# One attention and Fourier kernel on one core: array shapes chosen in the order, score units of four head groups, masks over 16 heads

## The chip, the core and the metric

The kernel runs on one core of a Trainium2 chip. The core has five engines that work side by side: TensorE (matrix products, called PE in the profile, its weight loads PEld), VectorE (DVE), ScalarE (ACT), GpSimd (POOL) and SyncE (SP), which here only issues DMAs. The metric is the time of one execution on the device in microseconds.

## The reference

One input x (2048 tokens, 640 channels) goes through two branches, and a gate per token mixes them. All tensors are bf16.

```python
H, N = 32, 4                      # 32 heads of 20 channels, 4 segments of 512 tokens
q, k, v = x @ wq, x @ wk, x @ wv  # cut into heads and segments
M = z = 0
for s in range(N):
    p = softmax(qs @ ks.T * 20 ** -0.5 + causal_mask)      # inside the segment
    a_dot = p @ vs
    a_mem = (phi(qs) @ M) / (phi(qs) @ z + 1e-6)           # memory of the segments before
    o = sigmoid(beta) * a_mem + (1 - sigmoid(beta)) * a_dot
    M, z = M + phi(ks).T @ vs, z + phi(ks).sum()           # phi(t) = t + 1 if t > 0 else exp(t)
a = concat(o) @ wo
b = irfft2(rfft2(x) * (w_r + 1j * w_i))
out = sigmoid((x * gate_w).sum(-1)) * a + (1 - the same) * b
```

## The kernel before

`record` writes down some 2,300 operations (products, copies, activations, masks, DMAs) with what they read and write. `schedule` then puts them into engine queues by a long list of numbers, `ORDER`: an entry v means operation v // 2 on its first or second possible engine (v % 2). So the sequence on every engine, and the engine of each operation that has two, is written out in that list. `schedule` also assigns the PSUM banks and the semaphore waits, with a cost model of its own.

*Stages.* For each segment s, `project` computes q, k (`proj_tile`: 128 channels by 512 tokens, five products of 128x128), v (`v_tile`), and the token gate; the rows of q and k go through memory (`st_qk`, `pad`) to get 20-row heads onto 32-row strips (`qkp`). `mem_read` reads the memory, `attend` does the attention, `mem_update` adds to the memory. `fft` is the Fourier branch: `F1`, `D`, `T`, `W_mul`, `W_add`, `Tb`, `Db`. `finish_tile` makes output tiles out of `Fb` and five `oproj`, and `final` copies them out of PSUM. The order list mixes all of these: Fourier products fill the places between attention products.

*Scores.* Eight groups of four heads per segment. A unit of scores (`qk_unit`) is a set of products into PSUM banks 0 to 3, all four of them, then one exponential on ScalarE (L1271; two for some units of segment 3) into the tile `ex`, then causal masks on GpSimd (L1292). Kind a is the first block of keys, kind b the next two, kind c the last. The units of two groups are a, b, a, c (of both), b: 20 units per segment. `ex` has three slots, so the scores of a group go to the slot of the group three before, after its product with v (`pvf` in segments 0 to 2, `pv` in segment 3). All other products use PSUM banks 4 to 7.

*Array shapes.* TensorE works as one array of 128x128, as four column tiles of 128x32 (`pvf`, `Fb`, odd v tiles, `projd`, output products), or as eight tiles of 20x64 (scores). The first is mode 0, the second 2, the third 1. In the profile's shapes these are `128*128`, `128*32` and `20*64`. Only the output products of segments 0 to 2 (`oproj`, mode -1) could take either of the first two, by their neighbours in the list.

*Lines.* L522 issues most products, L520 a product cut into four tiles; L531 and L533 are the copies out of PSUM on ScalarE and VectorE; L1080, L1092 and L1093 are phi; L1121 the gate's exponential; L1452 `W_add`; L1447 `W_mul`.

## Time and profile before

| | |
|---|---|
| median of 3 runs | 245.5 us (244.65 to 246.56) |
| the profiled execution | 246.08 us in all; span from first to last instruction 244.0 us |
| mean granted TensorE clock | 0.993 of full speed |
| TensorE / VectorE / ScalarE / GpSimd busy | 226.9 / 200.7 / 200.4 / 167.2 us |
| DMA | 42.17 MB, 173 GB/s on average |

In a row of a group, the form reads out<-in with partitions x elements; after the count come the busy time in us, the mean length of one in ns, and the idle time just before with what ended it. In a row of the time-ordered list come the start, the length, the engine, the line and how many instructions are merged. The lengths of products are modelled and overlap; their starts are measured. In a row of stages, after the bounds and the length, come the busy times of PE, PEld, DVE, ACT and POOL with instruction counts, the granted clock, the DMA share and GB/s.

### The profile page before, as it was taken

How to read it: one execution, taken by the hardware profiler on the slowest of the kernel's cores; microseconds unless marked ns; L12 is line 12 of the kernel's file. 1: busy time of each engine (PE TensorE's matmuls, PEld its weight loads, DVE VectorE, ACT ScalarE, POOL GpSimd, SP SyncE). 2: the span in 40 equal slices, each digit the busy share in tenths (PEclk: the TensorE clock that was granted, in tenths of full speed). 3: DMA queues.
4: the chain of work that ended last, by engine and by line, in shares of the span. 5: the costliest groups of instructions: out<-in, count | busy, mean ns of one | idle time of the engine just before them, and what ended most of it. 6: DMA issues, size and time to landing. Idle time of an engine off the chain costs nothing.

```text
span 244.0 us, 10261 instructions
## 1 busy us (share of the span) xinstructions
PE 226.9 (93%) x4349; PEld 140.8 (58%) x4361; DVE 200.7 (82%) x478; ACT 200.4 (82%) x243; POOL 167.2 (69%) x298
## 2 busy tenths in 40 slices
PE   7999999999979999899799979998999989999994
PEld 2674666766455665455575545565554546566793
DVE  0299989889999987999997998998999996735473
ACT  2388989988989999899898879999999968687801
POOL 8334069447959938649779895968898783857730
PEclk9999999999999999999999999999999999799999
DMA  7999959996977975849637583463876759382213
GB/s 168 301 330 268 209 173 182 233 194 199 214 209 131 189 222 147 183 141 252 159 98 203 134 247 97 126 169 105 227 172 201 182 130 206 95 87 83 72 67 108
DMA packets 58928, 42.17 MB, mean 173 GB/s; under 512 B 30020, under 2 KB 55172, under 8 KB 58884
## 3 DMA queue, kind: packets, MB, share of 16 engines
q1 hardware_dynamic: 57188, 40.71, 67.9%
q10 hardware_dynamic: 1696, 0.82, 1.2%
q8 instruction: 34, 0.56, 1.0%
q14 instruction: 10, 0.08, 0.1%
HBM read 23.32 MB, written 12.30 MB: 146 GB/s over the span
## 4 chain that ended last, share of the span: by engine, by line
PE 63%; DVE 16%; ACT 10%; DMA 7%; issue 2%; ACTq 0%; SPq 0%; DVEq 0%
PE psum L522 57%; ACT ex L1271 8%; PE psum L520 5%; DMA r<-r_scr 2%; DMA xT<-in_A_x_dram 2%; DVE Yt L1452 2%; DVE Pt L1447 2%; DVE phk L1093 2%; DMA dnc<-u_scr 2%; DVE oU L1534 1%; DMA u_scr<-ub 1%; ACT et L1080 1%; DVE Cp L533 1%; DVE ub L533 1%; DVE G L1493 1%
## 5 line engine op out<-in xcount | busy, mean ns | idle before, releaser
L1271 ACT ACTIVATE ex<-psum 128x2048 bf16<-128x2048 f32 (+4 forms) x92 | 138.6, 1506 | 15.5 <-PE psum L522 13.1
L1292 POOL TENSOR_SCALAR_AFFINE_SELECT ex<-ex 128x256 bf16<-128x256 bf16 (+2 forms) x224 | 122.6, 570 | 35.3 <-ACT ex L1271 32.8
L522 PE MATMUL psum<-qkp 20*64 20x64 bf16 (+5 forms) x1280 | 32.7, 271 | 3.9 <-ACT ex L1271 2.9
L522 PE MATMUL psum<-xT,wk 128*128 128x256 bf16 (+1 forms) x280 | 33.8, 281 | 0.6 <-DMA xT<-in_A_x_dram 0.4
L522 PE MATMUL psum<-wv,xT 128*32 128x320 bf16 (+3 forms) x400 | 29.4, 301 | 0.0
L522 PE MATMUL psum<-xT,wq 128*128 128x512 bf16 (+1 forms) x123 | 28.0, 385 | 0.8 <-issue 0.5
L1447 DVE TENSOR_TENSOR Pt<-psum,Wt 128x642 bf16<-128x642 f32 x32 | 25.5, 821 | 0.6 <-PE psum L522 0.2
L522 PEld LDWEIGHTS psum<-qkp 20*64 20x64 bf16 x1280 | 13.4, 103 | 21.6 <-ACT ex L1271 15.1
L522 PEld LDWEIGHTS psum<-xT,wk 128*128 128x128 bf16 (+1 forms) x280 | 19.8, 99 | 8.3 <-issue 1.8
L520 PE MATMUL psum<-wo,oU 128*32 128x320 bf16 x480 | 22.2, 305 | 0.5 <-DVE oU L1542 0.2
L522 PE MATMUL psum<-big,Ac 128*128 128x161 bf16 (+2 forms) x96 | 17.6, 257 | 2.0 <-DVE va L1123 1.5
L522 PE MATMUL psum<-ex,va 128*32 128x64 bf16 (+3 forms) x576 | 17.6, 257 | 1.8 <-DVE Pt L1447 1.3
L522 PE MATMUL psum<-big,Cp 128*128 128x321 bf16 (+1 forms) x96 | 18.1, 307 | 1.0 <-DVE G L1493 0.6
L522 PEld LDWEIGHTS psum<-wv,xT 128*32 128x32 bf16 (+1 forms) x400 | 14.5, 96 | 7.4 <-issue 2.0
L1123 DVE TENSOR_TENSOR va<-psum,ebx 128x320 bf16<-128x320 f32 x32 | 15.3, 483 | 2.9 <-PE psum L522 1.8
L914 POOL TENSOR_TENSOR xsb<-xf 128x320 bf16<-128x320 bf16 (+2 forms) x9 | 7.6, 846 | 14.4 <-DVE xsb L914 10.3
L522 PEld LDWEIGHTS psum<-ex,va 128*32 128x32 bf16 x576 | 11.0, 96 | 10.7 <-DVE Pt L1447 2.2
L1493 DVE TENSOR_TENSOR G<-eo,psum 128x320 bf16<-128x320 f32 x32 | 14.9, 478 | 2.3 <-PE psum L522 1.9
L533 DVE CAST ot<-psum 128x320 bf16<-128x320 f32 x18 | 8.5, 488 | 9.8 <-PE psum L520 7.9
L1080 ACT ACTIVATE et<-qu 128x512 bf16<-128x512 bf16 x25 | 15.3, 625 | 0.9 <-DVE phk L1093 0.9
L522 PE MATMUL psum<-tt,Yt 128*128 128x256 bf16 (+1 forms) x96 | 15.6, 274 | 0.3 <-DVE mem L1165 0.2
L1452 POOL TENSOR_TENSOR Yt<-Pt 128x321 bf16<-128x321 bf16 x17 | 12.7, 758 | 4.4 <-PE psum L522 3.9
(96 smaller groups left out, 401.2 us busy)
## 6 DMA issues: line engine op xcount, KB each, us to landing
qkp<-qk_scr SPq DMA_DIRECT2D x28, 160.0 KB
tt<-tab_tt SPq DMA_DIRECT2D x8, 512.0 KB, 4.3
qk_scr<-qu SPq DMA_DIRECT2D x12, 256.0 KB, 3.0
u_scr<-ub SPq DMA_DIRECT2D x12, 256.0 KB, 3.1
xsb<-in_A_x_dram SPq DMA_DIRECT2D x8, 320.0 KB, 4.9
oU<-u_scr SPq DMA_DIRECT2D x15, 128.0 KB, 3.2
out_dram<-ot SPq DMA_DIRECT2D x12, 160.0 KB
Wt<-in_B_w_r_dram SPq DMA_DIRECT2D x16, 80.2 KB, 3.2
```

The source lines that it names most:

```text
L520: h = e.matmul(dst, wt, r_, start=st, stop=sp_, **{**kw, "tile_position": (0, q), "skip_group_check": True})
L522: h = e.matmul(o_, l_, r_, start=st, stop=sp_, **kw)
L533: alts["dve"] = (lambda e: e.tensor_copy(dst(), src()), 67 + 1.04 * n, 68.0)
L914: self.either(lambda e, dst=dst, src=src, d0=d0, n=n, op=op: e.tensor_tensor(xs.ap(o + dst, [D, 2], [1, n]), xf.ap(src + d0, [321, 2], [1, ...
L1080: self.one("act", lambda e: e.activation(et.ap(0, [1, L]), qsl(), ACT.Exp), L, [qb], [b("et", pi_)], late, name="phi_exp")
L1093: fmin = lambda e: e.tensor_tensor(dst(), dst(), et.ap(0, [1, L]), ALU.min)
L1123: self.one("dve", lambda e: e.tensor_tensor(va.ap(i * H * VW + h0 * VW, [VW, nh], [1, DH]), self.ps(bank, 0, [DH, nh], [1, DH]), self.ebx. ...
L1271: self.one("act", lambda e, d=d, q=q: e.activation(self.ex.ap(*d), self.ps(bank, *q), ACT.Exp, scale=SC), n, [bank], [self.exb(s, 2 * pr + ...
L1292: self.one("pool", lambda e: e.affine_select(self.ex.ap(e0 + d0, [1280, 4], [1, n], np_=np_), self.ex.ap(e0 + s0, [1280, 4], [1, n], np_=np_),
L1447: self.one("dve", lambda e, ri=ri, Pt=Pt, Wt=Wt, wo_=wo_, bank=bank: e.tensor_tensor(Pt.ap(ri * 322, [644, 2], [1, KD]), self.ps(bank, 0, ...
L1452: fn = lambda e, r=r, a0=a0, a1=a1, op=op, Pt=Pt, Yt=Yt: e.tensor_tensor(Yt.ap(r * 322, [1, KD]), Pt.ap(a0 * 322, [1, KD]), Pt.ap(a1 * 322 ...
L1493: self.one("dve", lambda e, q=q, n2=n2, bank=bank, eo=eo: e.tensor_tensor(self.G.ap(n2 * D + 639 * q, [1 - 2 * q, 320]), eo.ap(q, [1, 320] ...
```

## The change

- *Array shapes.* Every full product gets a second form, `tiled`, four column tiles of 128x32, and the order list says which (an odd entry). In the new list 118 products are tiled: 35 `proj`, 30 `Db`, 15 `vproj`, 15 `D`, 10 `F1`, 5 `Tb`, 3 `memrd`, 3 `oT3`, 2 `T`. Output products are always tiled; those of segment 3 read their operand without a stride, and its copy out of PSUM writes with one.
- *Score units.* In segments 0 to 2 the last key blocks (kind c) of four head groups are one unit with one exponential of 128x2048, instead of two units of 128x1024: 18 units per segment. These blocks have places of their own, the "hole" in each of four slots of `ex`, one per group of a half; the rest of `ex` stays at three slots, and small tiles move into the gaps of the fourth.
- *Masks.* The three masks of kind c run once per four groups over 16 heads. A strip that is always zero is cleared once at the start (`clear`). One of the masks starts at partition 64 and has a semaphore wait on the GpSimd instruction before it, and the next one on it.
- *Smaller edits.* The gate column of odd v tiles becomes products of one column (`odd_gates`). phi runs once over two projection tiles where there are two. The reciprocal of the memory read covers both halves of the heads. `m_cp`, `m_mask` and the gate's copy may run on a second engine.
- *Order.* The cost model in `Sched` is replaced, and `ORDER` is a new list, searched with it (2,211 entries instead of 2,328). It moves operations on all engines.

```diff
 def mms(self, items, r, w, prio, name="", extra=0.0, mode=0):
...
-        op = self.Sc.op({"pe": (f, cost, 141.0)}, r=r, w=w, prio=prio, name=name, mode=mode)
+        four = [c for c in cols for _ in range(4)]
+        alts = {"pe": (f, *(pe_cost(cols, max(mode, 0)) if mode > -2 else pe_cost(four, 2)))}
+        if mode == -1:
+            alts["tiled"] = (f, *pe_cost(four, 2))
+        op = self.Sc.op(alts, r=r, w=w, prio=prio, name=name, mode=mode if mode > -2 else 2)
...
+    HALF = (((0,), 0), ((0,), 1), ((1,), 0), ((1,), 1), ((2,), 0), ((2,), 1), ((0, 1, 2, 3), 2), (0, -1), ((3,), 0), ((3,), 1), (1, -1), (2, -1), (3, -1))
...
-        self.ex = T("ex", [P, self.NEX * 4 * 1280])
+        self.ex = T("ex", [P, 4 * 5120])
...
+        clear = lambda e: e.memset(self.ex.ap(1216, [1280, 16], [1, 64], np_=64), 0.0)
+        self.Sc.op({"dve": (clear, 630, 94), "pool": (clear, 1054, 51)}, w=[self.hole(x, "m3") for x in range(4)], prio=0.0, name="clear")
...
+    def odd_gates(self, s, prio, xT, xb):
...
+        for i in (1, 3):
+            items = []
+            for c in range(5):
+                items.append((lambda i=i, c=c: (self.ps(bank, i // 2, [1, 1]), xT.ap(c * L + i * P, [1, P]), self.wv.ap(c * (D + 1) + D, [1, 1]),
+                                                c == 0, c == 4, {"skip_group_check": True}), 1))
+            self.mms(items, [b("gw"), bank] + xb, [], prio, name="gatep", mode=-1)
...
 def attend(self, s):
...
+            for half in range(2):
+                for u, (gps, kind) in enumerate(self.HALF):
+                    if kind < 0:
+                        self.pv_flipped(s, 4 * half + gps)
+                    else:
+                        self.qk_unit(s, 4 * half, u, (gps, kind))
...
 def pv_flipped(self, s, g):
...
-        self.mms(items, self.exall(s, g) + [b("va", s % 2, jj) for jj in range(4)] + [bank], [], prio, name="pvf", mode=2)
+        self.mms(items, self.exall(s, g) + [self.hole(g, k) for k in ("c0", "m3")] + [b("va", s % 2, jj) for jj in range(4)] + [bank], [], prio, name="pvf", mode=2)
...
+    def hole(self, g, k):
+        return self.b("hole", g % 4, k)
...
 def qk_unit(self, s, g0, u, unit):
...
-            outs = [((e0 + sh, [1280, 4], [step, 2], [1, 128]), (0, [512, 4], [128, 2], [1, 128]))]
+            outs = [((sh, [1280, 4], [5120, 4], [1, 128]), (0, [512, 4], [128, 4], [1, 128]))]
...
+        if s < 3 and kind == 2:
+            lo, hi = ([self.hole(x, k) for x in range(4)] for k in ("c0", "m3"))
+            self.mask("mask1216c", 0, 1216, 1088, 64, (0, 64), hi, prio, nh=16, r=lo, p0=64, np_=64)
+            self.mask("mask1088c", 0, 1088, 1088, 64, (0, 64), lo, prio, nh=16)
+            self.mask("mask1152b", 0, 1152, 1152, 64, (0, 64), lo, prio, nh=16, np_=64)
...
 -            self.mms(items, [b("w" + which + "a"), b("w" + which + "b"), xb[c], bank], [], prio, name="proj", mode=0)
+            self.mms(items, [b("w" + which + "a"), b("w" + which + "b"), xb[c], bank], [], prio, name="proj", mode=-1)
...
+                self.mms([(th, 320)], [b("oTl", c) if s == 3 else ob[c], wd(c), bank], [], prio, name="oproj", mode=-2)
```

The last edit but one stands for all full products: F1, D, T, Tb, Db, even v tiles, memrd, mupd, gateT and oT3 go from mode 0 to mode -1 in the same way.

542 lines of the change are left out of this document (285 added, 257 removed), and 189 rows, old and new, of the table ORDER.

## The prediction

> **What bounds the kernel now.** I read the page first, then the busy times by stage, then single instructions.
>
> ```profile
> span 244.0 us, 10261 instructions
> PE 226.9 (93%) x4349; PEld 140.8 (58%) x4361; DVE 200.7 (82%) x478; ACT 200.4 (82%) x243; POOL 167.2 (69%) x298
> PE 63%; DVE 16%; ACT 10%; DMA 7%; issue 2%; ACTq 0%; SPq 0%; DVEq 0%
> ```
>
> TensorE is busy for 93% and carries 63% of the chain that ended last, so it looks like the bound. Two busy times are not enough, though: three engines stand above 80%. So I cut the span where the score products of a new segment begin (the unit of kind b of its first head group), and once more where the last score exponential ends. The columns are the engines' busy times; the second answer holds only instructions on the tile `ex`, so its ACT column is the score exponentials alone.
>
> ```profile
> core 0: us, PE busy (x) PEld busy (x) DVE busy (x) ACT busy (x) POOL busy (x), PEclk, DMA share, GB/s
> 0.00:11.42 11.42, 9.76 (x142) 4.73 (x142) 1.06 (x3) 2.37 (x3) 6.70 (x11) 1.00 0.87 234
> 11.42:80.80 69.38, 66.74 (x1046) 42.65 (x1049) 65.66 (x168) 62.14 (x85) 43.12 (x79) 1.00 0.91 214
> 80.80:130.65 49.85, 46.75 (x839) 28.22 (x842) 46.28 (x111) 46.63 (x54) 35.40 (x68) 1.00 0.68 169
> 130.65:172.03 41.38, 38.18 (x694) 22.57 (x695) 36.97 (x72) 37.99 (x43) 34.31 (x64) 1.00 0.57 159
> 172.03:230.93 58.90, 55.81 (x1357) 33.80 (x1356) 43.30 (x110) 49.64 (x58) 44.80 (x77) 0.97 0.63 145
> 230.93:244.00 13.07, 9.63 (x286) 8.78 (x282) 7.43 (x17) 1.64 (x5) 2.90 (x5) 1.00 0.29 88
> ...
> 11.42:80.80 69.38, 4.38 (x144) 2.82 (x144) 34.12 (x21) 27.79 (x51) 1.00 0.91 214
> 80.80:130.65 49.85, 5.86 (x192) 3.60 (x192) 34.11 (x21) 29.50 (x55) 1.00 0.68 169
> 130.65:172.03 41.38, 5.12 (x168) 3.23 (x168) 29.36 (x17) 26.84 (x51) 1.00 0.57 159
> 172.03:230.93 58.90, 9.90 (x316) 8.55 (x317) 40.97 (x35) 37.16 (x68) 0.97 0.63 145
> ```
>
> All score units share PSUM banks 0 to 3, so a unit's products cannot start before the exponential of the unit before has been read out. That makes a chain: exponential, products, exponential. What one turn costs shows in the time-ordered list where ScalarE has nothing else to do.
>
> ```profile
> 150.56 1.88 ACT L1271 ACTIVATE ex<-psum 128x2048 bf16<-128x2048 f32 x1
> 152.49 0.43 PE L522 MATMUL psum<-qkp 20*64 20x512 bf16 x12
> 153.01 1.88 ACT L1271 ACTIVATE ex<-psum 128x2048 bf16<-128x2048 f32 x1
> 154.94 0.42 PE L522 MATMUL psum<-qkp 20*64 20x320 bf16 x16 [0.22 <-ACT ex L1271]
> 155.44 1.88 ACT L1271 ACTIVATE ex<-psum 128x2048 bf16<-128x2048 f32 x1
> ```
>
> The exponential ends at 152.44 and the next starts at 153.01: 0.57 us; the turn after it takes 0.55. The mean gap in a stage is its length less its exponentials, over its units (20, 20, 17 and 23 by the order list): (69.38-34.12)/20 = 1.76 us in segment 0, 15.7/20 = 0.79 in segment 1, 12.0/17 = 0.71 in segment 2, 17.9/23 = 0.78 in segment 3. Segments 1 and 2 sit close to the floor of 0.56: the score chain bounds them. Segment 0 sits far above it, so there something else does.
>
> TensorE's busy time can't say what, since its ends are modelled. I count its work from the order list and the rate at which instructions start.
>
> ```profile
> 28.27 0.59 PE L522 MATMUL psum<-xT,wq 128*128 128x512 bf16 x2
> ...
> 29.14 0.84 PE L522 MATMUL psum<-wv,xT 128*128 128x320 bf16 x5
> ...
> 228.71 1.95 PE L520 MATMUL psum<-wo,oU 128*32 128x320 bf16 x52
> 230.83 1.46 PE L522 MATMUL psum<-va,ex 128*128 128x21 bf16 x52
> ...
> 234.75 0.62 PE L522 MATMUL psum<-fcat,on 128*128 128x128 bf16 x8
> 235.30 1.45 PE L522 MATMUL psum<-wo,oTl 128*32 128x320 bf16 x36
> ...
> 238.35 2.21 PE L522 MATMUL psum<-wo,oTl 128*32 128x320 bf16 x60
> ```
>
> Five products of 320 columns take 0.84 us, a single one 0.30 (the modelled length), so one starts every 0.135 us; 512 columns take 0.21, 21 columns 0.025. A product cut into four column tiles starts a piece every (1.95-0.30)/51 = 0.032 us, 0.13 for the four: the shape itself costs nothing. A change of shape does: eight transposes at 0.057 us end at 235.20, the tiled products begin at 235.30, 0.10 later. The order list has 216 such changes. Products and changes then make 64.5 us in segment 0 (of 69.4), 44.3 in segment 1 (49.9), 35.3 in segment 2 (41.4), 52.7 in segment 3 (58.9), and 8.6 in the tail, where the last 60 pieces end at 240.56, 9.6 us in. So TensorE bounds segment 0 and, with a granted clock of 0.97, most of segment 3 and the tail.
>
> **The change, part by part.** I numbered the operations of the changed program in the order in which its functions record them, and read its order list with that.
>
> Array shape in the order: 118 full products are now tiled, but the changes of shape go from 216 to 213. At 0.10 us that is 0.3 us, and 40 new one-column products of `odd_gates` cost 40 x 0.025 = 1.0 us. TensorE's total stays: 211.8 before, 211.2 after. What changes is where it lies: start 6.4 to 7.4, segment 0 64.5 to 60.1, segment 1 44.3 to 44.2, segment 2 35.3 to 37.7, segment 3 52.7 to 52.2, tail 8.6 to 9.7. Work leaves the stage that TensorE bounds for one where it has 6 us to spare.
>
> The weight loads of tiled pieces:
>
> ```profile
> L522 PEld LDWEIGHTS psum<-xT,wk 128*128 128x128 bf16 (+1 forms) x280 | 19.8, 99 | 8.3 <-issue 1.8
> L522 PEld LDWEIGHTS psum<-wv,xT 128*32 128x32 bf16 (+1 forms) x400 | 14.5, 96 | 7.4 <-issue 2.0
> ```
>
> A quarter load lasts as long as a full one (96 against 99 ns) and there are four, but at 0.13 us for four pieces they lie beside the products. The Trainium skill, TensorEngine Tiling (Array Packing), Tile-to-Partition Mapping, says that column tiling switches off fast weight loading, which speaks against this change; the trace shows no loss at 320 columns.
>
> Fewer exponentials and masks, by these rows:
>
> ```profile
> L1271 ACT ACTIVATE ex<-psum 128x2048 bf16<-128x2048 f32 x56 | 105.1, 1877 | 7.2 <-PE psum L522 5.5
> L1080 ACT ACTIVATE et<-qu 128x512 bf16<-128x512 bf16 x25 | 15.3, 625 | 0.9 <-DVE phk L1093 0.9
> L1271 ACT ACTIVATE ex<-psum 128x1024 bf16<-128x1024 f32 x12 | 12.3, 1024 | 1.7 <-PE psum L522 1.4
> L1121 ACT ACTIVATE gate<-psum 64x1 f32<-64x1 f32 x16 | 2.6, 165 | 0.5
> L1292 POOL TENSOR_SCALAR_AFFINE_SELECT ex<-ex 128x256 bf16<-128x256 bf16 x128 | 60.1, 480 | 29.7 <-ACT ex L1271 28.4
> L1292 POOL TENSOR_SCALAR_AFFINE_SELECT ex<-ex 64x512 bf16<-64x512 bf16 x64 | 43.4, 683 | 5.3 <-ACT ex L1271 4.4
> L1292 POOL TENSOR_SCALAR_AFFINE_SELECT ex<-ex 128x512 bf16<-128x512 bf16 x32 | 22.4, 703 | 0.3
> L1452 POOL TENSOR_TENSOR Yt<-Pt 128x321 bf16<-128x321 bf16 x17 | 12.7, 758 | 4.4 <-PE psum L522 3.9
> ```
>
> - ScalarE: 12 exponentials of 1.024 us become 6 of 1.877, 12.3 to 11.3 us; each segment below 3 has 18 units instead of 20. phi: 30 of 0.625 become 6 of 0.625 and 12 over 1024 columns; with the slope (1877-1024)/1024 = 0.83 ns these take 1.05, so 18.8 becomes 16.4. The 16 half-height gate exponentials become 4. Evictions shift to VectorE. By the list ScalarE falls 4.2 us in segment 0 and 2.8 in segment 1.
> - GpSimd: 48 masks of 0.480 and 24 of 0.683 go (39.4 us); 18 over 16 heads come, 1024 elements, by the slope (703-480)/256 = 0.87 ns 703+446 = 1.15 us, 20.7 in all. The list gives part back: `W_add` on GpSimd 17 to 24 times (0.758 each). Worth nothing directly: GpSimd mostly waits for the exponentials (28.4 us of its idle time before one form alone).
> - VectorE gives up those seven `W_add`, merges phi and the reciprocals of the memory read, and takes evictions. By the list it falls by 11 us in segment 0, where it is busy 65.66 of 69.38 us, and 5 of these go to the start; in segment 2 it gains 5, beside a score chain that is longer. No cost, as long as that chain leads.
> - DMA: 231 issues on SP before and after, none larger. The memset `clear` runs on VectorE in the start, where it is busy 1.06 of 11.42 us: nothing.
>
> The added wait: the four-group unit's three masks must all run before any `pvf` of its half. `pvf` stands in TensorE's queue, and products behind it wait too; the exponential that reuses the group's slot waits for it. One `pvf` of before, for its length:
>
> ```profile
> 170.87 0.73 PE L522 MATMUL psum<-ex,va 128*32 128x512 bf16 x24
> ```
>
> Per half GpSimd takes 3 x 1.15 = 3.4 us after the exponential. In five of six halves the list places two exponentials (2 x 2.4 us) or more before the one that needs the slot: covered. In the last half of segment 2 only one stands there. Its successor (segment 3's first, which writes the slot of head group 5) waits for three masks, one more of 0.5, and two `pvf`, 1.2 in a row: 5.1 us, against 0.56+1.88+0.56 = 3.0 without a wait, so 2.1 late. TensorE has Fourier products around it; I charge 0.5, between 0 and 2.1.
>
> The sum, on the profiled execution (246.08 us in all, span 244.0, 2.1 around it): start +0.2 (two more projections before the first score; 0 to 1.0). Segment 0 -3.2: TensorE loses 4.4 and ScalarE 4.2, both must go for the stage to shrink, and I take three quarters (0 to -4.4). Segment 1: 34.1 to 18 x 1.877 = 33.8, and two turns of 0.56 go: -1.4 (0 to -1.9). Segment 2: 14 x 1.877 + 3 x 1.024 + 17 x 0.71 = 41.4 against 16 x (1.877+0.71) = 41.4: 0. Segment 3: its chain loses 1.6, TensorE 0.5; between them -1.0, with the late exponential -0.5 (1.1 to -1.6). Tail +1.1, since TensorE has seven more output products after the last `pv` (0 to 1.1). Together -3.8. The profiled execution stands 0.6 above the median of 245.5, so the same step from the median gives **241.7 us**. The lower ends of the parts add to -7.9, 237.6; the upper ones to +3.2, 248.7.
>
> **The rivals.**
> *Nothing moves.* TensorE's total is 211.8 against 211.2 us, so if it bounds everywhere, freed ScalarE and GpSimd time becomes idle time: 245.5-0.6 = 244.9. The 63% share speaks for it; the 6 us between 35.3 and 41.4 in segment 2, and the gap of 0.57 repeated there, against it. The Trainium skill, TensorEngine Tiling (Array Packing), Key Properties, says that a change of tiling mode drains TensorE; the 0.10 us above agrees, and it is the rule by which this rival keeps its cost, as the number of changes hardly falls.
> *Slower: the 16-head masks.* If GpSimd runs late in every half as in the last of segment 2, the slot wait costs 2.1 us six times, of which 0.5 is charged: 241.7+12.6-0.5 = 253.8. It decides from the point where the third mask ends more than about 4 us after its exponential. GpSimd's idle share (31%) speaks against it.
> *Slower: weight loads show.* If four loads of 96 ns can't hide behind a product, 0.384-0.136 = 0.25 us on 118 products: 29 us, 271. The 52 pieces in 1.95 us speak against it.
>
> **How the numbers follow.** Forecast 0.60 (237.6 to 243), nothing moves 0.24, masks 0.14, loads 0.02. A measurement of this kernel tells about 1% (2.5 us) from no change. Faster 0.60, within 1% 0.24, slower 0.16. The range takes the forecast's lower bounds, a little more for what a denser order may win (236.5), and reaches past the second case to 247.0; all upper ends at once, and the masks, are left out.
>
> **What would show it.** Right: 74 score units; segment 0 near 66 us, segment 1 near 48.5, the tail near 14; gaps between exponentials unchanged near 0.6 in the middle; GpSimd's busy time near 156. Wrong: segment 0 still 69 us (TensorE waits on VectorE or a DMA there); gaps over 1 us in front of exponentials whose slot is read by a late `pvf`; masks far above 1.15 us; a longer stretch of granted clock below 1, which the last third has now.

## The result and the profile after

The changed kernel takes 255.5 us (median of four executions, 253.8 to 257.3) where the kernel before takes 245.3 (244.7 to 246.6): 1.041 times as long, with an interval of 1.032 to 1.050. The forecast was 241.7. The profiled execution took 257.27 us, 255.5 of it in the span. Executions of one kernel differ by several us, some of them by stretches of lower granted clock, and the ratios leave out the slow ones (over 1.5% above the kernel's fastest) while the medians take in all.

The head of the page of the changed kernel:

```profile
span 255.5 us, 11230 instructions
PE 233.2 (91%) x4895; PEld 144.1 (56%) x4905; DVE 204.2 (80%) x443; ACT 196.6 (77%) x206; POOL 165.4 (65%) x251
PE 63%; DVE 13%; POOL 9%; ACT 8%; issue 3%; DMA 2%; SPq 0%; DVEq 0%
```

GpSimd is at 9% of the chain that ended last, where it did not appear before. ScalarE is 4 us less busy, GpSimd 2, VectorE 3 more and TensorE 6 more. That alone does not say where 11 us more come from. The stages do, cut at the same units as before (stage, length, busy times, clock, DMA):

```profile
0.00:16.29 16.29, 12.88 (x148) 5.59 (x149) 4.63 (x11) 1.88 (x3) 5.90 (x10) 1.00 0.95 247
16.29:82.23 65.94, 63.32 (x1144) 40.94 (x1149) 59.52 (x131) 57.72 (x68) 45.72 (x63) 1.00 0.85 199
82.23:131.13 48.90, 46.46 (x947) 29.13 (x948) 45.56 (x99) 44.55 (x40) 37.31 (x58) 1.00 0.75 175
131.13:175.90 44.77, 42.34 (x942) 25.59 (x944) 39.79 (x82) 37.96 (x36) 32.18 (x48) 1.00 0.57 163
175.90:238.14 62.24, 56.03 (x1352) 33.78 (x1353) 46.24 (x108) 47.88 (x56) 43.15 (x73) 0.92 0.60 127
238.14:255.50 17.36, 12.12 (x380) 9.10 (x368) 8.42 (x17) 6.60 (x6) 1.18 (x3) 1.00 0.27 77
```

| stage | before | forecast | after | after less before |
|---|---|---|---|---|
| start, to the first exponential | 11.42 | 11.6 | 16.29 | +4.87 |
| segment 0 | 69.38 | 66.2 | 65.94 | -3.44 |
| segment 1 | 49.85 | 48.45 | 48.90 | -0.95 |
| segment 2 | 41.38 | 41.4 | 44.77 | +3.39 |
| segment 3 | 58.90 | 58.4 | 62.24 | +3.34 |
| tail | 13.07 | 14.2 | 17.36 | +4.29 |

Segments 0 and 1 came out as forecast; the loss is at the start, in segments 2 and 3, and in the tail. The score units are 74, as forecast. The clock column shows where TensorE was granted less than its full clock: 0.92 on the average in segment 3. Three things in the trace stand where the time went. First, all instructions that write the tile `oTl` (lines with the smallest, middle and largest length in ns: ScalarE's and VectorE's after the change, then VectorE's before it), and the places of these copies in the chain that ended last, after the change (start, length, engine, tile):

```profile
L553 ACT ACTIVATE oTl<-psum x2: 2423/2466/2509, 240.7 to 245.5; 128x512 bf16<-128x512 f32 x2
...
L554 DVE CAST oTl<-psum x3: 2406/2406/2481, 226.1 to 245.7; 128x512 bf16<-128x512 f32 x3
...
L533 DVE CAST oTl<-psum x5: 679/691/692, 213.4 to 235.8; 128x512 bf16<-128x512 f32 x5
...
226.06 2.41 DVE oTl L554
...
234.93 2.33 DVE oTl L554
...
240.66 2.43 ACT oTl L553
...
245.58 2.44 ACT oTl L553
```

Before, the same five copies of 128x512 took 0.679 to 0.692 us. Four of the five now stand in that chain with 9.6 us; four of 0.69 us would be 2.8. Second, the start, in the time-ordered lists of TensorE and of SP's queue, after the change and then before it:

```profile
1.30 4.02 PE L542 MATMUL psum<-G 128*128 128x512 bf16 x9 [1.30 <-DVE G L831]
7.43 0.62 PE L542 MATMUL psum<-xT,wk 128*32 128x256 bf16 x8 [2.10 <-DMA xT<-in_A_x_dram]
7.83 1.07 PE L542 MATMUL psum<-xT,wq 128*32 128x512 bf16 x8
...
0.78 0.40 SPq L577 DMA_DIRECT2D xsb<-in_A_x_dram  x1
1.24 5.42 SPq L575 DMA_TRANSPOSE xT<-in_A_x_dram  x3
...
5.68 1.05 PE L522 MATMUL psum<-xT,wk 128*32 128x256 bf16 x16 [0.36 <-DMA xT<-in_A_x_dram]
...
0.78 4.31 SPq L554 DMA_TRANSPOSE xT<-in_A_x_dram  x3
```

A load of x rows now stands ahead of the three transposing loads; these take 5.42 us to issue instead of 4.31, the first product on `xT` starts at 7.43 instead of 5.68, and TensorE idles 2.10 us. Third, the place at the end of segment 2 that the prediction had marked, in the lists of ScalarE, TensorE and GpSimd:

```profile
170.79 1.88 ACT L1326 ACTIVATE ex<-psum 128x2048 bf16<-128x2048 f32 x1
...
175.90 1.24 ACT L1326 ACTIVATE ex<-psum 128x1280 bf16<-128x1280 f32 x1 [1.73 <-PE psum L542]
...
173.62 0.42 PE L542 MATMUL psum<-qkp 20*64 20x320 bf16 x16
174.55 1.28 PE L542 MATMUL psum<-ex,va 128*32 128x512 bf16 x48 [0.51 <-POOL ex L1355]
...
170.29 5.88 POOL L1355 TENSOR_SCALAR_AFFINE_SELECT ex<-ex 64x1024 bf16<-64x1024 bf16 x6 [0.58 <-ACT ex L1326]
```

The scores of segment 3's first unit (3b0) are there at 174.0, its exponential starts at 175.90: it waits for the two value products at 174.55, which free its buffer, and these wait for the 16-head masks. Between two exponentials lie 3.23 us instead of 0.58.

### The profile page after: what moved, and what is told of

Same layout as the page of the kernel before. It is cut to its first block, busy times and chain, and to the rows that moved or that the text cites. A ratio compares the mean times of both kernels' runs of the same rounds, so it can differ in the third digit from the quotient of the medians.

```text
span 255.5 us, 11230 instructions
## 1 busy us (share of the span) xinstructions
PE 233.2 (91%) x4895; PEld 144.1 (56%) x4905; DVE 204.2 (80%) x443; ACT 196.6 (77%) x206; POOL 165.4 (65%) x251
## 4 chain that ended last, share of the span: by engine, by line
PE 63%; DVE 13%; POOL 9%; ACT 8%; issue 3%; DMA 2%; SPq 0%; DVEq 0%
PE psum L542 50%; PE psum L540 13%; POOL ex L1355 9%; ACT ex L1326 5%; DMA xT<-in_A_x_dram 2%; ACT oTl L553 2%; DVE oTl L554 2%; DVE Pt L1511 1%; DVE va L1161 1%; DVE Yt L1516 1%; DVE qu L554 1%; DVE Ac L554 1%; DVE Cp L554 1%; DVE xsb L942 1%; DVE phq L1119 1%
## 5 line engine op out<-in xcount | busy, mean ns | idle before, releaser
L1326 ACT ACTIVATE ex<-psum 128x2048 bf16<-128x2048 f32 (+3 forms) x86 | 137.5, 1599 | 19.5 <-PE psum L542 17.5
L1355 POOL TENSOR_SCALAR_AFFINE_SELECT ex<-ex 128x256 bf16<-128x256 bf16 (+4 forms) x170 | 111.8, 675 | 40.4 <-ACT ex L1326 37.6
L542 PE MATMUL psum<-xT,wk 128*128 128x256 bf16 (+1 forms) x240 | 28.6, 302 | 2.3 <-DMA xT<-in_A_x_dram 2.1
L542 PE MATMUL psum<-xT,wq 128*128 128x512 bf16 (+1 forms) x110 | 24.5, 433 | 0.5 <-issue 0.2
L542 PEld LDWEIGHTS psum<-qkp 20*64 20x64 bf16 x1280 | 13.9, 104 | 19.3 <-ACT ex L1326 12.7
L1516 POOL TENSOR_TENSOR Yt<-Pt 128x321 bf16<-128x321 bf16 x24 | 17.7, 753 | 8.2 <-PE psum L542 5.4
L542 PEld LDWEIGHTS psum<-xT,wk 128*128 128x128 bf16 (+1 forms) x240 | 16.6, 106 | 9.9 <-DMA xT<-in_A_x_dram 3.0
L554 DVE CAST ot<-psum 128x320 bf16<-128x320 f32 x16 | 7.7, 490 | 13.9 <-PE psum L540 13.8
L540 PEld LDWEIGHTS psum<-wo,oU 128*32 128x32 bf16 x480 | 13.2, 102 | 7.1 <-issue 2.9
L542 PE MATMUL psum<-big,Ac 128*128 128x161 bf16 (+2 forms) x81 | 14.4, 256 | 0.2
L554 DVE CAST Cp<-psum 65x256 bf16<-65x256 f32 (+1 forms) x25 | 13.3, 541 | 1.3 <-PE psum L542 0.7
L1112 ACT ACTIVATE et<-qu 128x1024 bf16<-128x1024 bf16 (+1 forms) x15 | 13.6, 906 | 0.2
```

Of the source, the lines that this page charges most:

```text
L540: h = e.matmul(dst, wt, r_, start=st, stop=sp_, **{**kw, "tile_position": (0, q), "skip_group_check": True})
L542: h = e.matmul(o_, l_, r_, start=st, stop=sp_, **kw)
L554: "dve": (lambda e: e.tensor_copy(dst(), src()), round(67 + 1.04 * n) + spread // 3, 94)}
L1112: self.one("act", lambda e: e.activation(et.ap(0, [1, n_el]), qt.ap(po, [1, n_el]), ACT.Exp), n_el, rb, ebuf, late, fix=97, name="phi_exp")
L1326: self.one("act", lambda e, d=d, q=q: e.activation(self.ex.ap(*d), self.ps(bank, *q), ACT.Exp, scale=SC), n, [bank], dst, prio - self.QK_L ...
L1355: self.one("pool", lambda e: e.affine_select(self.ex.ap(e0 + dst, [1280, nh], [1, n], p0=p0, np_=np_), self.ex.ap(e0 + src, [1280, nh], [1 ...
```

## The experiments

Theory: three separate losses, the strided copy (7 to 8 us), the start (5), the late unit (2 to 3). Rival: the new order leaves TensorE idle as it is, and these places are only where it shows. Every run was timed beside the kernel before on the same chip, but not all on one chip, so across the rows the ratios compare better than the medians; the stage lengths are those of the one profiled execution.

| run | median, us | ratio to before (interval) | start | seg. 0 | seg. 1 | seg. 2 | seg. 3 | tail |
|---|---|---|---|---|---|---|---|---|
| neighbouring copy | 248.46 | 1.014 (0.995 to 1.032) | 16.33 | 68.68 | 49.25 | 44.31 | 58.16 | 13.77 |
| before, strided copy | 252.30 | 1.031 (1.015 to 1.048) | 11.33 | 69.71 | 49.93 | 41.37 | 57.40 | 19.06 |
| start order | 254.31 | 1.036 (1.013 to 1.060) | 13.99 | 68.52 | 49.17 | 44.29 | 61.36 | 17.27 |
| copy and start order | 249.27 | 1.016 (0.999 to 1.033) | 14.24 | 65.48 | 49.50 | 45.09 | 59.56 | 13.93 |
| the same, folds behind | 249.58 | 1.022 (1.019 to 1.025) | 12.24 | 69.21 | 48.89 | 44.72 | 59.56 | 13.38 |
| copy, warming products | 248.85 | 1.021 (1.015 to 1.027) | 13.52 | 67.10 | 49.10 | 45.93 | 57.54 | 13.41 |
| copy, full shapes | 251.81 | 1.027 (1.020 to 1.034) | 15.29 | 67.29 | 49.66 | 44.64 | 58.74 | 13.68 |
| copy, start order, copies on ScalarE ("mended") | 248.32 | 1.011 (1.004 to 1.019) | 12.86 | 67.51 | 48.88 | 44.66 | 58.83 | 13.56 |
| mended, two masks cut | 245.06 | 0.999 (0.994 to 1.004) | 12.23 | 66.88 | 48.07 | 43.75 | 60.17 | 13.70 |

In segment 0 the first and the third row hold a stretch of lower clock of some 3 us, which the others don't.

### The copy

```diff
-  copy: oTl.ap(c * L, [1, 32], [32, 16]) <- psum
+  copy: oTl.ap(c * L, [1, L]) <- psum
-  oproj, segment 3: weights oTl.ap(c * L + a * P, [1, P])
+  oproj, segment 3: weights oTl.ap(c * L + 4 * a, [1, 4], [16, 32])
```

> The changed kernel with one edit: the copy of the last transposes into oTl writes 512 neighbouring elements again, and the output product of segment 3 reads its weights 16 elements apart, as before the change; the order is the changed one, entry by entry. Theory A (the strided write is the cost): each of the five copies takes 0.6 to 0.8 us instead of 2.3 to 2.4, segment 3 ends 3 to 4 us earlier and the tail is 13 to 14.5 us instead of 17.4, the granted clock near 228 to 232 us no longer falls, and the time is 246 to 249.5 us, 6 to 9 us under the changed kernel's 255.5. Rival B (the order is the cost: TensorE is left idle in segment 3 whatever the copy takes, and the lower clock follows): the copies shrink all the same, but the time falls by less than 2.5 us and the clock still falls to 0.5 to 0.6 in two stretches of segment 3.

The reverse, one part of the change done alone on the kernel before:

```diff
-  copy: self.oTl.ap(c * L, [1, L])
+  copy: self.oTl.ap(c * L, [1, 32], [32, 16])
-  oproj, segment 3: self.oTl.ap(c * L + 4 * a + q, [16, 32])
+  oproj, segment 3: self.oTl.ap(c * L + 32 * (4 * a + q), [1, 32])
```

> The kernel before the change with the strided copy alone: the copy into oTl puts the tokens of one column quarter side by side, and the output product of segment 3 reads 32 neighbouring elements. Theory A: the five copies take 2.3 to 2.45 us instead of 0.69 and the time rises by 3 to 8 us, to 248 to 253, all of it behind the first copy, in segment 3 and the tail; the start and segments 0 to 2 stay within 0.3 us. Rival B (the copies have room beside other work, and the read of neighbouring weights gives something back): the time stays within 1.2 us of 245.3.

The `oTl` rows (as above) and the last two stages of the first; then VectorE's copies, the two rows of TensorE's waits on them, and the tail of the second:

```profile
L559 ACT ACTIVATE oTl<-psum x2: 597/597/597, 238.0 to 241.8; 128x512 bf16<-128x512 f32 x2
...
L560 DVE CAST oTl<-psum x3: 682/691/693, 227.6 to 242.0; 128x512 bf16<-128x512 f32 x3
...
178.57:236.73 58.16, 53.66 (x1383) 33.47 (x1382) 42.81 (x109) 47.88 (x56) 43.73 (x73) 1.00 0.66 136
236.73:250.50 13.77, 10.52 (x343) 9.65 (x340) 6.55 (x17) 2.87 (x6) 1.16 (x3) 1.00 0.34 96
```

```profile
L533 DVE CAST oTl<-psum x5: 2394/2412/2606, 211.4 to 238.6; 128x512 bf16<-128x512 f32 x5
...
  PEld psum L522: 4.4, 3
  PE psum L522: 3.4, 3
...
229.74:248.80 19.06, 10.34 (x286) 7.46 (x282) 13.97 (x17) 1.53 (x4) 2.89 (x5) 1.00 0.20 58
```

Theory A holds both ways. Without the stride the changed kernel loses 7.1 us (255.5 to 248.5; 6.7 by the two ratios). In the profiled executions segment 3 is 4.1 shorter, with a clock of 1.00 instead of 0.92, and the tail 3.6. With the stride, the kernel before gets 5.5 us longer (246.8 to 252.3; 7.7 by the ratio); between the profiled executions the tail grows by 6.0 (13.07 to 19.06), while segment 3 is 1.5 shorter at a clock of 1.00 instead of 0.97. Of the 4.1 us in segment 3, 2.7 stand ahead of one unit, behind the copy at 226.06: its exponential waits 3.42 us in the changed kernel and 0.69 without the stride. Another 1.2 stand ahead of the first of these copies, where the changed kernel's clock fell to 0.50 between 212 and 216 us; they are not the copy's. The lower clock of segment 3 in the changed kernel went with the copy in this execution; the mended kernel shows 0.94 there again, so the clock is not the copy's alone.

What the layout was for can be read off, too, from the weight loads that read `oTl`, first of the run with neighbouring copies (strided read), then of the changed kernel:

```profile
L539 PEld LDWEIGHTS psum<-wo,oTl x160: 135/138/152, 240.0 to 246.8; 128*32 128x32 bf16 x160
...
L540 PEld LDWEIGHTS psum<-wo,oTl x160: 92/97/97, 243.7 to 252.0; 128*32 128x32 bf16 x160
```

A load without a stride is 0.041 us shorter, 160 times, beside products; the tail with strided loads and dense copies is 3.6 us shorter all the same.

### The start

One entry of the order moved, the first load of x rows behind the three transposing loads:

```diff
-  SP: ld_x, xT, xT, xT, ld_wkb, ...
+  SP: xT, xT, xT, ld_x, ld_wkb, ...
```

> The changed kernel with one entry of the order moved: the first load of x rows goes behind the three transposing loads on SP's queue instead of ahead of them. Theory A (the late transposes leave TensorE idle for 2 us at 5.3 to 7.4 us, and its products then run at half speed up to 13 us): the first product on xT starts at 5.7 to 6.2 us, the first exponential at 11.3 to 12.5 us instead of 16.3, and the time falls by 4 to 5 us, to 250.5 to 251.5. Rival B (the start is slow because its products are all in the 32-column shape, or because wk comes ahead of wq): the first product starts earlier by 1.5 us, but the first exponential stays at 14.5 us or later and the time falls by 0.5 to 1.8 us.

Then both edits together, where the sum was to show:

> Both edits together on the changed kernel: the copy writes neighbouring elements, and the first load of x rows stands behind the transposing loads. If the two causes are separate (theory A on both), the gains add up: 10.5 to 13.5 us under the changed kernel, 242 to 245 us, level with the kernel before or up to 3 us under it. If one of them is covered by the other or by the order (rival B on either), the gain is under 8 us and the time stays over 247.5.

TensorE and VectorE in the start of the kernel with the order alone:

```profile
6.04 0.40 PE L542 MATMUL psum<-xT,wk 128*32 128x256 bf16 x8 [1.17 <-DMA xT<-in_A_x_dram]
...
12.48 0.39 PE L542 MATMUL psum<-xT,wk 128*128 128x256 bf16 x2 [1.69 <-DVE qkp L554]
...
8.91 0.50 DVE L937 TENSOR_TENSOR xf<-xsb 128x640 bf16<-128x640 bf16 x1 [7.66 <-DMA xsb<-in_A_x_dram]
...
11.74 0.68 DVE L554 CAST qkp<-psum 128x512 bf16<-128x512 f32 x1
```

Both expectations missed by size. The products start at 6.04 and run at full speed (eight pieces of 256 columns in 0.40 us, not 0.62), but now TensorE waits 1.69 us for VectorE's copies, which stand behind folds of the x rows that came later. So the early load of x rows was the other side of an order that puts the folds first. The time fell by 1.2 us (255.5 to 254.3) and, beside the mended copy, not at all (248.5 to 249.3).

Moving the folds behind these copies, with one copy on ScalarE:

```diff
-  DVE: fold, fold, fold, fold, fold, copy, copy, copy
+  DVE: copy, copy, fold, fold, fold, fold, fold      ACT: copy
```

> The kernel with both earlier edits (neighbouring copy, x rows behind the transposing loads) and, on VectorE, the five folds of the first x rows moved behind the three copies of the first q and k projections, the first of which goes to ScalarE. Theory C (in the run with the start order mended, the copies at 11.7 to 13.3 us stood behind folds that waited for the x rows, and TensorE sat idle for 1.7 to 2.0 us behind them): TensorE does not wait at 10.8 us, the first exponential is at 11.3 to 12.3 us instead of 14.0 to 14.2, and the time falls by 2 to 3 us against the run without this edit (249.3), to 246 to 247.5. Rival D (the start is not on the path that sets the end: segment 0 waits for the folds and their products instead): the first exponential is as early, but segment 0 is longer by as much, and the time stays within 1 us of 249.3.

The start is 12.24 as theory C said, and segment 0 takes it back (69.21; 249.6 us), as rival D said. Giving the copies to ScalarE and leaving the folds early:

```diff
-  DVE: fold x5, copy, copy, copy
+  DVE: fold x5      ACT: copy, copy, copy
```

> The changed kernel with the neighbouring copy and the x rows behind the transposing loads, the folds left early on VectorE, and the first three copies of the q and k projections given to ScalarE, which has nothing to do until the first exponential. Theory C2 (the start and segment 0 are one chain, in which the copies of the first projections, the folds and the later copies on VectorE follow one another: moving the folds behind the copies gave 2.0 us at the start and took 3.7 us back in segment 0): with the copies out of VectorE's queue, the first exponential is at 11.2 to 12.4 us and the first unit of segment 1 at 77.5 to 78.8 us (79.7 with the copies on VectorE and early folds), the time 1 to 2.2 us under that run. Rival D (segment 0 ends by its own chain of TensorE work and does not follow the start): the first unit of segment 1 stays at 79.2 to 80.5 us, the time within 0.8 us.

The first exponential is at 12.86, later than theory C2 had it, and the first unit of segment 1 at 80.37 (before: 80.80; forecast: 77.8), as rival D had it; the time, 1.0 us under the run with both edits (1.2 by the ratios), would fit C2, but the intervals overlap. One execution says little here: eight more runs below have the same start and segment 0, with edits in segment 2 only, and their first unit of segment 1 comes at 78.2 to 80.6 us, the middle of all nine at 79.8. In the runs with both edits, with the folds moved, with more warming products (the next run) and mended, the first exponential stands at 14.24, 12.24, 13.52 and 12.86 us, and the fifth at 33.99, 35.00, 34.49 and 33.95. In these four an earlier start gains nothing at the fifth unit, and in the eight further runs, with starts of 12.2 to 13.9, it stands anywhere from 32.4 to 34.2. What holds it is not shown by a run; in the trace ScalarE's queue has five copies of `Ac` (the Fourier branch's first products, made from the folds) ahead of that exponential, three of which, in the run with the folds moved, wait 0.49 to 1.46 us for TensorE.

Whether the idle time made the products slow, tested without moving a load: five more warming products behind the ninth.

```diff
-  warm product k: [one product of 512 columns]
+  warm product k: [one product of 512 columns] * (6 if k == 8 else 1)
```

> The changed kernel with the neighbouring copy and its own start order, and five more warming products of 512 columns behind the ninth, which keep TensorE at work from 5.3 to 7.4 us while the transposing loads are late; nothing else. Theory G (the 2.1 us of idling are what made the products from 7.4 to 13 us run at half speed, though the profile gives the granted clock there as 1.00): the products on xT run at full speed from 7.5 us (four of 256 columns in 0.40 to 0.45 us, not 0.62), the first exponential is at 13.2 to 14.3 us instead of 16.3, and the time falls by 2 to 3 us against the run with the copy mended (248.5), to 245.5 to 246.5. Rival H (the slowness is of the products or of their operands' arrival, not of the idling): they stay at half speed, the first exponential stays at 15.5 us or later, and the time is within 1 us of 248.5.

```profile
1.30 5.28 PE L548 MATMUL psum<-G 128*128 128x512 bf16 x14 [1.30 <-DVE G L837]
7.33 0.40 PE L548 MATMUL psum<-xT,wk 128*32 128x256 bf16 x8 [0.76 <-DMA xT<-in_A_x_dram]
7.56 0.60 PE L548 MATMUL psum<-xT,wq 128*32 128x512 bf16 x8
```

Theory G holds for the mechanism: same transposing loads, same products, 0.40 instead of 0.62 us and 0.60 instead of 1.07, the first exponential at 13.52 instead of 16.33. Nine products in 4.02 us are 0.45 each (0.21 at full speed), so TensorE was still slow when it fell idle, and after the idle time it stayed slow until about 13 us. The Trainium skill, TensorE: Matmul & The Clock Gate, Part 1, says that TensorE runs at half its clock until it has been busy for a window of about 3.4 us, and that these windows run free of the kernel's start; the rows agree with the half rate, while the profile's clock column says 1.00 throughout. Where the slow stretch falls differs from run to run: with the same idle time of 2.11 us, the run with full shapes (below) has its products at full speed from 7.43 us (0.40) and at half speed from about 8.9 to 12.4, and there the clock column shows it, at 0.50. The time did not follow in the run with more warming products (248.85 against 248.46, on another chip; 1.021 against 1.014 by the ratios): nothing gained, as above.

### The late unit and the masks

Unit 3b0 trades places with unit 2a7, on the kernel with the folds moved:

```diff
-  qk: 2b6, 3b0, [pvf 2.4, 2.5], 2a7     exp: 2b6, 3b0, 2a7
+  qk: 2b6, 2a7, [pvf 2.4, 2.5], 3b0     exp: 2b6, 2a7, 3b0
```

> The run before this in the list with one more edit: the score unit 3b0 and its two exponentials trade places with the unit 2a7, so that 3b0 no longer stands at the place where it waits for the products on the values of head group 4 and these for the 16-head masks. Theory E (the wait of 2.1 us between the exponentials near 173 us is a loss of its own, as the prediction placed it): the gap of 3.2 us there goes down to 0.6 to 1.2 us and the time falls by 1.5 to 2.5 us against the run with the folds moved. Rival F (the loss moves on: 2b7 or 3b0 waits at its new place, or TensorE is the bound there): the gap goes, one of 1.5 us or more comes within the next four units, and the time falls by less than 0.7 us or rises.

The gap is 2.68 us at 2a7 and 1.18 at 3b0: 2a7 writes the slot that `pvf` of group 4 frees, so the wait only changes its owner. The four times spread from 247.8 to 256.4 (median 250.6) and tell nothing. Rival F, as to the gap; as to the time, open.

The combined unit one place earlier, its masks at the head of GpSimd's queue:

```diff
-  exp: 2b5, 2c4567      POOL: mask 2b5, gate product, M1216, M1088, M1152b
+  exp: 2c4567, 2b5      POOL: M1216, M1088, M1152b, mask 2b5, gate product
```

> The run before this in the list with one more edit: in segment 2 the combined unit of head groups 4 to 7 trades places with unit 2b5 on TensorE and ScalarE, and its three 16-head masks go ahead of the masks of 2b5 on GpSimd, one unit or 2.5 us earlier than the order has them. Theory E2 (unit 3b0 and before it 2a7 wait for the buffer that the value products of groups 4 and 5 free, and these for three masks of 1.36 us in a row): the gap of 3.2 us ahead of 3b0 goes down to 0.6 to 1.5 us, segment 2 is 1.5 to 2.5 us shorter (44.8 to 42.5 to 43.3) and so is the time. Rival F (TensorE's own work sets the end of segment 2, 37.7 us of it by the prediction against 35.3 before): the gap goes but others grow, segment 2 stays within 0.6 us of 44.8.

> The run before this in the list, and unit 3b0 trades places with 2a7 as in the earlier run of that edit. Theory E2: with the masks early, 2a7 needs only the value products of group 4 and 3b0 comes when those of group 5 are long done, so that no gap over 1.2 us is left around 170 us: 0.3 to 1.0 us under the run with the early masks. Rival F: no gain over the early masks alone, within 0.4 us.

Both missed, in the other direction: 255.3 and 253.2 us, a gap of 9.3 and 8.8 us. In the first, in the lists of VectorE and TensorE:

```profile
167.55 1.33 DVE L1031 TENSOR_SCALAR gate<-gate 128x4 f32<-128x4 f32 x1
172.73 0.17 DVE L1206 SCALAR_TENSOR_TENSOR dn<-psum,ebg 128x16 f32<-128x16 f32 x1 [3.85 <-POOL ebg L1034]
...
174.93 1.79 PE L548 MATMUL psum<-big,Cp 128*128 128x321 bf16 x6 [4.48 <-DVE mem L1216]
```

A gate product of 0.4 us on GpSimd stood behind three masks of 1.36 us; VectorE waited 3.85 us for it and TensorE 4.48 us for VectorE. With only the first mask moved ahead of it:

> The mended kernel with the combined unit of groups 4 to 7 of segment 2 one unit earlier on TensorE and ScalarE, and on GpSimd only the first of its three masks ahead of the mask of 2b5 and of the small gate product, which held up VectorE and TensorE in the earlier attempt. Theory E2 (late masks): the gap of 3.1 us ahead of unit 3b0 goes down to 1.0 to 2.0 us and segment 2 is 1 to 2 us shorter. Theory W: the gap goes down, but the time comes back in other gaps before or behind it, segment 2 and the time change by less than 0.6 us. Third case: the gate product is late again, a gap of over 3 us appears between 168 and 176 us and the time is 2 us or more longer.

Third case again: a gap of 6.3 us, segment 2 at 47.8, 249.4 us in all. The masks are not simply late in the order: of the places tried, none on GpSimd is better.

So I took the masks away instead of moving them:

```diff
-  mask1088c: nh=16      mask1152b: nh=16
+  mask1088c: nh=4       mask1152b: nh=4
```

> The first kernel of this list with two of the three masks of each combined unit cut from 16 heads to 4 (the masks of the other 12 heads are left out, so part of the computation is missing): 0.9 us less for each on GpSimd, twelve times. Theory M (the 16-head masks are late in one place alone, ahead of unit 3b0): that gap of 3.2 us becomes 1.3 to 1.7 us, nothing else moves by 0.6 us, the time falls by 1.3 to 2 us. Rival N, the prediction's slower case (they are late in every half): each of the six halves gains 1 to 1.8 us and the time falls by 6 to 10 us. Rival F (TensorE is the bound): the time falls by less than 0.6 us.

The time falls by 3.3 us, to 245.1 (by 1.5 between the two profiled executions, since segment 3 is 1.3 longer in this one): more than M said, less than N. It comes in small pieces (segment 1 is 0.8 shorter, segment 2 0.9; the 0.6 of segment 0 are less than that stage varies by itself), and the gap ahead of 3b0 only goes from 3.07 to 2.63. There TensorE no longer waits for the masks, and the value products still come where its queue has them:

```profile
169.23 0.42 PE L548 MATMUL psum<-qkp 20*64 20x320 bf16 x16
169.58 1.28 PE L548 MATMUL psum<-ex,va 128*32 128x512 bf16 x48
```

The exponential of 3b0 needs the end of both, at 170.86, and starts at 170.93. The order places them behind the scores of the unit that waits for them: 1.3 of the 2.6 us are built into the list.

### What sets segment 2

With all masks and no edit aimed at it, it was 44.3 to 45.9 us long, 2.9 to 4.5 longer than before. Work of one engine was added or taken away in this stage alone, on the mended kernel. These kernels leave a part of the computation out or do a part of it several times.

```diff
+  vproj, segment 3: the second of five products issued four times
```

> The changed kernel with the three mends of the copy, the start order and the first copies on ScalarE (in the following: the mended kernel, 248.3 us, segment 2 44.7 us), and in the eight value projections of segment 3, which run during segment 2, the second of five products issued four times instead of once (its share is counted four times): 24 products of 320 columns at 0.136 us, 3.3 us of TensorE work more. Theory W (TensorE's work sets the length of segment 2): it grows by 2.3 to 3.5 us and the time by 2 to 3.5. Rival S (the chain of score units sets it, as the prediction had it, and TensorE's 7 us of idle time there take the work up): it grows by less than 1 us.

```diff
+  vproj, segment 3: w = 32 columns in two of five products
```

> The mended kernel with two of the five products of these eight value projections cut from 320 columns to 32 (most of their share of the values of segment 3 is left out): sixteen times 0.115 us, 1.8 us of TensorE work less in segment 2. Theory W: segment 2 is 1.2 to 1.9 us shorter and the time falls by 1 to 1.9 us. Rival S: segment 2 changes by less than 0.5 us.

```diff
+  exp, segment 2, kinds a and b: 256 columns of each head instead of 512
```

> The mended kernel with the exponentials of all score units of segment 2 but the two combined ones cut to half their columns (the other half of the weights is left as it was in an earlier segment): fourteen times some 0.85 us less on ScalarE, 12 us of the score chain. Rival S (the chain of score units sets the length of segment 2): it is 7 to 12 us shorter. Theory W (TensorE's work does): it is shorter by 0 to 2.5 us, the gaps between the exponentials grow from 0.55 to over 1.2 us on the average, and the time falls by less than 2.5 us.

```diff
+  W_mul, groups 10 to 15: [644, 2], [1, 161] instead of [644, 2], [1, 321]
```

> The mended kernel with the twelve multiplications on VectorE that fall into segment 2 (the spectral products of the last six of sixteen groups) cut from 642 columns to 322 (the other half of the products is left as an earlier group wrote it): twelve times 0.4 us, 4.8 us less of VectorE's 39.9 us in segment 2. Theory V (VectorE, busy 89% of segment 2, sets its length, alone or by turns with TensorE): segment 2 is 1.5 to 4.5 us shorter than 44.7 and the time falls by 1 to 4 us. Theory W2 (TensorE alone does, and the cut of 1.8 us missed it only by its place): segment 2 changes by less than 0.8 us. Rival P (a chain through the gates and GpSimd's masks fixes the pace of the last ten units): less than 0.8 us, and the gaps of the last six units stay as they are, to 0.1 us.

> The cut of VectorE work and the earlier cut of TensorE work together (4.8 us and 1.8 us of segment 2; both leave out the same parts of the computation as before). Theory V: 2.5 to 5.5 us shorter than 44.7, more than either alone. Theory W2: about 1 to 1.8 us shorter. Rival P: segment 2 changes by less than 0.8 us, with the gap of 3 us ahead of unit 3b0 unchanged.

Segment 2 in the stage view, in this order: the mended kernel, its instructions on `ex` alone, more TensorE work, less TensorE work, half exponentials, these on `ex` alone, less VectorE work, less of both:

```profile
129.25:173.91 44.66, 42.55 (x943) 25.78 (x944) 39.89 (x82) 37.87 (x35) 32.10 (x48) 1.00 0.56 163
129.25:173.91 44.66, 5.67 (x192) 3.57 (x192) 0.00 (x0) 30.03 (x16) 26.08 (x37) 1.00 0.56 163
...
127.04:173.43 46.39, 45.15 (x1003) 28.33 (x1004) 40.09 (x82) 38.03 (x36) 31.35 (x48) 1.00 0.55 154
128.31:172.85 44.54, 40.62 (x943) 24.67 (x944) 39.83 (x82) 37.91 (x36) 32.08 (x48) 1.00 0.57 163
129.02:173.83 44.81, 42.16 (x943) 25.83 (x944) 40.08 (x82) 26.97 (x36) 31.74 (x48) 1.00 0.60 161
129.02:173.83 44.81, 5.67 (x192) 3.58 (x192) 0.00 (x0) 18.07 (x17) 25.56 (x37) 1.00 0.60 161
128.37:172.72 44.35, 41.91 (x942) 25.78 (x944) 37.32 (x82) 37.76 (x35) 32.23 (x48) 1.00 0.60 164
129.29:173.45 44.16, 39.91 (x942) 24.79 (x944) 37.19 (x82) 37.75 (x36) 32.18 (x48) 1.00 0.58 164
```

Exponentials go from 30.03 to 18.07 us and the stage stays (44.66, 44.81): rival S, on which the prediction rested, falls for this kernel; on the kernel before it was not tested. TensorE work from 42.55 to 40.62 changes the stage by 0.1, less VectorE work by 0.3, both cuts together by 0.5; 3.3 us more of TensorE work by 1.7. These are single executions, and without an edit the stage varies by 1.6 us, so only the 12 us of exponentials and, just, the 1.7 us say much. Theory V falls, and so does W for the cut; the added work speaks for a part of it. Rival P, a chain through the gates and GpSimd's masks, is left standing: it allowed less than 0.8 us, and the gap ahead of 3b0 stays (3.23 and 3.25 against 3.07), though two other late gaps shrink by 0.18 where it allowed 0.1. Whether such a chain or the other engines together hold the stage, no run shows. The medians don't settle it either: 253.8, 247.0, 250.5, 246.9 and 247.3 us, against 248.3; the first and the third spread by 8 us.

What can be read off is the sum. The stage less its exponentials is the gaps: 41.38-29.36 = 12.0 us before, 44.66-30.03 = 14.6 mended. Of the 2.6 us more, 2.5 are the one gap ahead of 3b0 (0.58 to 3.07); it is 2.6 to 4.1 us in every run that leaves the order around it alone. No run removed that gap without another in its place, so that the 3.3 us come from it is read, not shown.

### The array shapes

All 118 products that the order had tiled, back in the full shape (on the kernel with the neighbouring copy):

```diff
-  ORDER: 118 odd entries ("tiled")
+  ORDER: the same entries, even ("pe")
```

> The changed kernel with the neighbouring copy, and all 118 products for which the order had chosen four 32-column pieces back in the full shape; the order of all instructions stays. TensorE's queue then changes shape 261 times instead of 213. Theory I (the choice is worth its switches, 0.10 us each): 48 more switches are 4.8 us of TensorE time, of which some lies beside other waits: the time rises by 1.5 to 4.8 us against 248.5. Rival J (the shape does not matter within the noise, because TensorE waits at most of these places): the time stays within 1.2 us of 248.5. Rival K (pieces of 32 columns cost more than a full product, whatever the switches): the time falls by more than 1.2 us.

251.8 us, a ratio of 1.027 against 1.021 and 1.022 of two relatives on the same chip and 1.014 of its own base on another: 1.2 to 3.3 us longer, theory I at its lower end, with intervals that overlap. In this order the chosen shapes are perhaps worth a little; the order before had as few changes of shape (216) without them.

## Why the prediction was wrong

The forecast's stages add up to 240.2 us of span; the mended kernel has 246.3, the changed one 255.5. The largest step that failed is a term that the sum put at nothing without a reason, the copy with a stride; next is the gain at the start and in segment 0 that did not come. By the steps of the sum:

- **A term that was missing: the copy with a stride.** The list of edits had it, the sum had no row for it. Five copies of 0.69 us became 2.4 to 2.5, four of them on the chain that ended last. Worth 7.1 us taken away and 5.5 put in alone. The tail, charged with +1.1 for seven output products, was +4.3; without the stride, in the rows above, it is 13.4 to 13.9, under the 14.2 forecast, and segment 3 is 57.5 to 60.2 around 58.4. Both terms were otherwise about right.
- **Start, +0.2 (0 to 1.0): mis-sized, +4.9.** I counted products and the DMA issues ("231 before and after") but not the order of those issues, though a moved step counts with each queue that it passes. Some 1 to 4 us of it reach the first unit of segment 1 (82.23 against 78.2 to 81.5 in the runs with a mended start); what reaches the end doesn't show in the medians (248.3 to 249.6, against 248.5 with the late start).
- **Segment 0, -3.2: right number, wrong reason.** After a late start the stage is short; with the start mended it is 65.5 to 69.2 us long, 67.5 in the mended kernel, -1.9. Start and segment 0 together gained 0.4 us in the mended kernel and 1.0 in the middle of the nine runs with its start (79.8 against 80.8), not 3.0. That three quarters of TensorE's and ScalarE's relief would show was the failed step; what holds segment 0 instead is not shown.
- **Segment 1, -1.4: about right**, -0.95.
- **Segment 2, 0, with 0.5 charged for a wait of 2.1: the wait was right, the charge wrong.** The place, the slot, the masks and the length (2.1 forecast, 2.65 measured) were as worked out. But the exponential that waits stands on the chain itself: no score products can go ahead of it, since all units share four PSUM banks. Other products on TensorE fill TensorE's time, not the chain's. By this reading the whole 2.1 had to be charged; no run shows it, and half the exponentials without a shorter stage speak against reckoning this segment by the score chain alone.
- **Masks, 1.15 us by a slope: 1.36 and 1.41 measured** as the means of the two shapes. The third ended 4.3 to 8.4 us after its exponential, past the 4 us from which the prediction's slower rival decides. The rival took 2.1 us for each half; cutting two of the three masks gave 3.3 us in all by the medians. It was there, at about a quarter of its price; that its 253.8 us lie near the measured 255.5 is luck, since the copy made up the difference.
- **The rivals.** With copy and start mended, 248.3 us is 1.1% over the kernel before (0.4 to 1.9%): not the forecast's gain, and slower than "nothing moves" had it (244.9). Six units fewer gave no time that the runs show, and in segment 2 cutting 12 us of exponentials gave none. Weight loads did not show: with the 118 products back in the full shape the time was no shorter.
- **What would show it:** 74 units, segments 0 and 1 near 66 and 48.5, as said. The tail of 17.4 us and GpSimd's 165 us missed the 14 and 156 named for being right, and of the signs named for being wrong, masks over 1.15 us, a gap over 1 us ahead of an exponential behind a late `pvf`, and a lower clock in the last third came.

No run beat the kernel before; 245.1 us with part of the masks left out equals it.

## What to carry to other kernels

Give every edit in the list a row of the sum, and look first at those that change an access pattern: a stride that saves 0.04 us on hidden weight loads can cost 1.7 us on a copy that others wait for. When a wait sits on the chain that you have named as the bound, charge all of it, unless a row shows what covers it on that chain. A shorter stage after a late start is no gain, so add up stages from the beginning before calling a part of a forecast right, and when several engines are 85 to 95% busy, don't expect relief of one to shorten anything.

## What the hardware showed

- A copy of 128x512 from PSUM took 0.597 us on ScalarE and 0.691 on VectorE with neighbouring bf16 written, 2.42 to 2.55 and 2.39 to 2.61 when neighbours were written 64 bytes apart: four and three and a half times as long. Reading with such a stride from PSUM cost nothing; the copies of `ub` in the changed kernel do that (on VectorE):

```profile
L554 DVE CAST ub<-psum x16: 628/682/692, 48.6 to 176.0; 128x512 bf16<-128x512 f32 x16
```

  So the layout with neighbouring tokens could be had by a strided read and a dense write; that was not tried. The Trainium skill, SBUF — State Buffer, Door 1: The DMA port swizzle, has the rule that accesses which leave a 16-byte line each time pay for it, and that a stride is free up to 8 bf16; 32 here, and these rows agree.
- A small VectorE operation stretched while one of GpSimd's masks ran: the 128x4 `gate` operation took 0.16 us in the kernel before, 0.52 in the mended one and 1.33 in the run quoted above, and in all three it ended 0.03 to 0.04 us behind the mask that was running when it started.
- After 2.1 us without work at the start TensorE ran at half speed for more than 5 us in the changed kernel, in a stretch for which the profile's clock column says 1.00, and for some 3.4 us in the run with full shapes, where the column says 0.50; in the run with more warming products, with 0.76 us without work, it ran at full speed at once.
